# Attention visits of one unit or of two: eight heads of 256 tokens at a time from block 2 on

## The chip, the cores and the metric

The kernel runs on one core of a Trainium2 chip. Its time is the device time of one launch in microseconds (us); where several runs were timed, the median is given. A profile shows one further execution, with the start and length of each engine's instructions. The engines are TensorE (PE, with its weight loads PEld), VectorE (DVE), ScalarE (ACT), GpSimd (POOL) and SyncE (SP, which here only issues DMAs).

## What is computed

Four sequences of 768 tokens go through a retention layer of 8 heads of 64, and its output, as 3072 rows of 512, through a two-layer net with a leaky activation whose slope is learned per column.

```python
def _attn_ref(q, k, v):
    gamma = 1.0 - 2.0 ** (-5.0 - np.arange(H))
    scale = 1.0 / np.sqrt(D)
    for t in range(S):
        state = gamma[None, :, None, None] * state + np.einsum('bhd,bhe->bhde', k[:, :, t], v[:, :, t])
        y[:, :, t] = scale * np.einsum('bhd,bhde->bhe', q[:, :, t], state)

def _moe_ref(x, w_in, w_out, alpha):      # x: [3072, 512], w_in: [512, 2048], w_out: [2048, 512]
    h = x @ w_in
    g = np.maximum(h, 0.0) + alpha * np.minimum(h, 0.0)
    return g @ w_out
```

## The kernel before

**Blocks and units.** The 3072 rows are cut into 6 blocks of 512 (`n`, 0 to 5). The retention is cut into 24 *units* `w`: 256 tokens (`u = w // 2`) of four of the eight heads (`g = w % 2`: heads 0 to 3, or 4 to 7). Four units make a block. A unit has two chunks `c` of 128 tokens. `c3` is the place of the 256 tokens in their sequence (0, 1, 2).

**The dense work of a block.** `ffn1(n)` makes the first product: 16 groups of four dense products of 128x512 (L438); each group has a PSUM bank of its own, and `minus` (ScalarE, L418) and `prelu` (VectorE, L407) turn it into a 128x512 piece of `gt`. Then `ffn2(n)` makes the second: four groups of 16 products (L461), each copied out by ScalarE (`os`, L475) and written to memory by a DMA on SP's queue (L481). Both are Python generators that yield after each product, and `tick(gen, m)` emits `m` of them. The program is thus one hand-written order; the engines run their own queues in that order and wait for each other by semaphores.

**A visit.** While `ffn2(n)` runs, the retention of block n + 1 is put between its products in *visits*. `visit(w_old, w_new)` finishes one unit and begins another:

- `within(w_old)`: 16 small products (64x64 quarters of the array) of the masked scores `m2` with v into `y` (L352); then the *carried* products that add the state's share where row half and chunk are the same (L330); then a bell: a VectorE memset of one element (L365) that tells that these are through, because the other row half writes the same bank next.
- `scores(w_new)`: 16 small products of q with k into `sc` (L267); `state_sums(w_new)`: 16 (8 in the last chunk pair of a sequence) of k with v into two banks, one for each chunk (L292).
- `finish(w_old)`: the other carried products (L330), which wait for the bell; ScalarE copies y to `xT`, the next block's input (L381, 128x512).
- VectorE: `masked` multiplies the scores with the causal mask (L303, 128x1024); `state` adds the decayed state and decays again (L317, L319, 128x128 each), one pair for each chunk.

In blocks 2 to 4 there are four visits in each `ffn2`, after 16, 30, 44 and 57 of its 64 products; in block 1 there is one more, `visit(None, 8)`, after two. Block 0 has an order of its own, and block 5 has no next block.

**Preparation.** `ahead()` prepares the next unit: GpSimd scales k and q and casts v (L191, L211), SP issues the transposing DMA that gives `kq` (L204, units 8 to 23), and SP issues the loads of the unit four further on (L151). These queues keep the program's order too.

**PSUM.** Eight banks of 128x512: two "dense" banks in turn (`f`: fa, fb), two for the sums in turn (`p`: pa, pb), a pair for the scores (`s`), a pair for `y`. A unit uses half of the y pair (columns 256 to 768). `ffn1` goes round all eight in the order of a string such as "fspyfSpY"; `ffn2` uses fa and fb in turn.

Of the kernel before, what the change touches and what calls it, by code (L numbers as in the profile page):

```python
# [18 lines left out]
def kernel(  # L19
# [15 lines left out]
    nc = tc.nc  # L35
# [7 lines left out]
    WB = 4  # L43
# [96 lines left out]
    def place(w):  # L140
        u, g = divmod(w, 2)
        b, c3 = divmod(u, NUS)
        return u, g, b, c3
# [111 lines left out]
    def half(i):  # L255
        return slice(64 * i, 64 * i + 64)
# [23 lines left out]
    def chunks(w):  # L280
        return (0,) if place(w)[3] == NUS - 1 else (0, 1)
# [17 lines left out]

    def masked(w):  # L300
        kdq, kq, vx, sc = live[w]
        m2 = sbp.tile([128, 4, 2, 128], F16, tag="m2", bufs=2, name="m2")
        nc.vector.tensor_tensor(  # L303
            out=m2.rearrange("p s a i -> p s (a i)"),
            in0=sc.rearrange("p (s n) -> p s n", n=256),
            in1=mask.unsqueeze(1).to_broadcast([128, 4, 256]),
            op=MULT,
        )
        live[w][3] = m2

    def state(w, cs=None):
        u, g, b, c3 = place(w)
        decay = tab[:, 32 + 2 * g : 34 + 2 * g].unsqueeze(2).to_broadcast([128, 2, D])
        for c in cs or chunks(w):
            stv = sums.pop((w, c))[:, 0:128].rearrange("p (x e) -> p x e", e=D)
            if c3 + c > 0:
                nc.vector.tensor_tensor(out=stv, in0=tgs[2 * u + c, g], in1=stv, op=ADD)  # L317
            tg = sbp.tile([128, 4, D], F16, tag="tg", bufs=8, name="tg")[:, 0:2, :]
            nc.vector.tensor_tensor(out=tg, in0=stv, in1=decay, op=MULT)  # L319
            tgs[2 * u + c + 1, g] = tg  # L320

    def carried(w, y, started, same, after=None):
        u, g, b, c3 = place(w)
        kq = live[w][1]
        for x in range(2):
            for r in range(2):
                c = r if same else 1 - r
                if c3 + c == 0:
                    continue
                ins = nc.tensor.matmul(  # L330
                    out=y[half(x), 256 + 256 * c + 128 * r : 384 + 256 * c + 128 * r],
                    lhsT=tgs[2 * u + c, g][half(r), x, :],
                    rhs=kq[half(r), 4 + 2 * x : 6 + 2 * x, half(c)],
                    start=(c, x) not in started,
                    stop=(same == (c == r)),
                    skip_group_check=True,
                )
# [6 lines left out]
    def within(w, mid=None, teller=None, pair="y"):  # L344
        u, g, b, c3 = place(w)
        vx, m2 = live[w][2:4]
        y = ps("y", pair, 1024, FP, 1)
        started = set()
        for r in range(2):
            for a in range(2):  # L350
                for c, x in DIAG:
                    nc.tensor.matmul(  # L352
                        out=y[half(x), 256 + 256 * c + 128 * r : 384 + 256 * c + 128 * r],
                        lhsT=vx[half(c), 2 * r + x, a, :],
                        rhs=m2[half(c), 2 * r + x, a, :],
                        start=(c, x) not in started,
                        stop=(a == 1 and c3 + c == 0),
                        skip_group_check=True,
                    )
                    started.add((c, x))  # L360
        if mid:
            mid()
        last = carried(w, y, started, True)
        if teller != nc.scalar:
            done = (teller or nc.vector).memset((warm if teller is None else bell)[0:1], 0.0)  # L365
        else:
            done = teller.activation(
                out=word[0:1], in_=word[0:1], func=COPY, bias=0.0, scale=1.0
            )
        behind(done, last, "tells that the products within the chunks are through")  # L370
        live[w].append((y, started, done))

    def finish(w):
        u, g, b, c3 = place(w)
        y, started, done = live[w].pop()
        carried(w, y, started, False, done)
        live.pop(w)
        n, i = divmod(u, 2)
        if w % WB == 0:
            xT[n] = sbp.tile([128, 2, 4, 2, 128], F16, tag="xT", bufs=2, name=f"xT{n}")  # L380
        nc.scalar.activation(  # L381
            out=xT[n][:, g, 2 * i : 2 * i + 2].rearrange("p c r (i a) -> p (c r) i a", a=2),
            in_=y[:, 256:768].rearrange("p (s a i) -> p s i a", a=2, i=64),
            func=COPY,
            bias=0.0,
            scale=1.0,
        )

    def visit(w_old, w_new, cs=None, tag="p", early=False):
        if w_old is not None:  # L390
            within(w_old)
        if w_new is not None:
            scores(w_new)
            state_sums(w_new, cs, tag)
        if w_old is not None:
            finish(w_old)
        if w_new is not None and early:
            state(w_new, cs)
        if w_new is not None:
            masked(w_new)  # L400
        if w_new is not None and not early:
            state(w_new, cs)

    gts = {}

# [15 lines left out]
    def ffn1(n, order="spyfSpYf", lead=(0, 0)):  # L421


        gt = sbp.tile([128, NFT, TB], F16, tag="gt", bufs=2, name=f"gt{n}")
        gts[n] = gt
        banks = Banks(order)
        hpss = {}
        narrow, wide = lead
        steps = [(ft, hp, 0, 2) for ft in range(narrow) for hp in range(NP)]
        for hps in ((0, 1), (2, 3)):  # L430
            steps += [
                (ft, hp, 2 if ft < narrow else 0, 4) for ft in range(wide) for hp in hps
            ]
        steps += [(ft, hp, 0, 4) for ft in range(wide, NFT) for hp in range(NP)]
        for ft, hp, lo, hi in steps:
            if hp == 0 and ft not in hpss:
                hpss[ft] = banks.next("hps")
            nc.tensor.matmul(  # L438
                out=hpss[ft][:, 128 * lo : 128 * hi],
                lhsT=w_in_all[:, hp, 128 * ft : 128 * ft + 128],  # L440
                rhs=xT[n][:, hp // 2, lo:hi, hp % 2, :],
                start=(hp == 0),
                stop=(hp == NP - 1),
            )
# [41 lines left out]
    def tick(gen, m):  # L486
        for _ in range(m):
            if next(gen, 1) == 1:
                return
# [198 lines left out]
```

## Time and profile before

| | |
|---|---|
| median of three runs | 212.56 us (212.12, 212.56, 214.99) |
| the profiled execution, its own time | 211.06 us |
| its span | 209.3 us |
| instructions | 5212 |
| data moved by DMA | 38.27 MB, mean 183 GB/s |

The span is the time from the first to the last profiled instruction; a little lies around it. The profile's page gives busy times, the busy share in 40 slices, the chain of waits that ended last, and the costliest groups of instructions. The timeline lists instructions in order, those of one kind merged: start, length, engine, line, operation, names, shape and count, and in brackets the engine's idle time ahead of them and what ended it. Matmuls overlap and their ends are modelled, so distances are best taken from start to start.

### The profile page before, as it was taken

How to read it: one execution, taken by the hardware profiler on the slowest of the kernel's cores; microseconds unless marked ns; L12 is line 12 of the kernel's file. 1: busy time of each engine (PE TensorE's matmuls, PEld its weight loads, DVE VectorE, ACT ScalarE, POOL GpSimd, SP SyncE). 2: the span in 40 equal slices, each digit the busy share in tenths (PEclk: the TensorE clock that was granted, in tenths of full speed). 3: DMA queues.
4: the chain of work that ended last, by engine and by line, in shares of the span. 5: the costliest groups of instructions: out<-in, count | busy, mean ns of one | idle time of the engine just before them, and what ended most of it. 6: DMA issues, size and time to landing. Idle time of an engine off the chain costs nothing.

```text
span 209.3 us, 5212 instructions
## 1 busy us (share of the span) xinstructions
PE 202.2 (97%) x2135; PEld 101.1 (48%) x2135; DVE 126.2 (60%) x225; ACT 97.3 (47%) x166; POOL 72.9 (35%) x97
## 2 busy tenths in 40 slices
PE   7989999999999999999999999999999999999993
PEld 2655454554444555444555444555444554444452
DVE  2783986465688736688347688346788433588000
ACT  2674763274765223665223665223665223665121
POOL 0578889389945563544022454000000000000000
PEclk9999999999999999999999999999999999999999
DMA  6999999999999994991184993314500111100112
GB/s 189 336 373 359 347 397 374 369 294 312 338 280 250 229 320 114 243 318 38 53 243 114 227 285 92 99 54 107 150 0 3 50 53 50 53 0 0 50 54 96
DMA packets 64119, 38.27 MB, mean 183 GB/s; under 512 B 19152, under 2 KB 57568, under 8 KB 64096
## 3 DMA queue, kind: packets, MB, share of 16 engines
q1 hardware_dynamic: 63632, 37.69, 61.8%
q8 instruction: 16, 0.26, 0.5%
q10 hardware_dynamic: 464, 0.25, 0.5%
q14 instruction: 7, 0.06, 0.1%
HBM read 27.45 MB, written 6.29 MB: 161 GB/s over the span
## 4 chain that ended last, share of the span: by engine, by line
PE 89%; SPq 4%; DMA 3%; DVE 1%; ACT 1%; issue 1%; POOL 0%; DVEq 0%
PE hps L438 40%; PE ops L461 40%; SPq L151 4%; PE y L352 3%; DMA wi<-in_moe_w_in_dram 3%; PE sc L267 2%; PE y L330 2%; PE st L292 1%; PE trb L239 1%; DVE m L303 1%; ACT kq L245 0%; ACT os L475 0%; POOL win L181 0%; DVE tg L319 0%; DVE st L317 0%
## 5 line engine op out<-in xcount | busy, mean ns | idle before, releaser
L461 PE MATMUL ops<-wout,gt 128*128 128x512 f16 (+1 forms) x400 | 88.5, 371 | 0.3 <-ACT os L475 0.3
L438 PE MATMUL hps<-xT,win 128*128 128x512 f16 (+1 forms) x392 | 84.8, 375 | 0.3 <-POOL win L181 0.3
L407 DVE SCALAR_TENSOR_TENSOR gt<-hm,oma,hps 128x512 f16<-128x512 f32 x96 | 71.2, 747 | 21.3 <-ACT hm L418 11.6
L418 ACT ACTIVATE hm<-hps 128x512 f32<-128x512 f32 x96 | 57.0, 597 | 24.9 <-PE hps L438 24.4
L438 PEld LDWEIGHTS <-win 128*128 128x128 f16 x392 | 37.9, 98 | 45.1 <-POOL win L181 0.5
L461 PEld LDWEIGHTS <-gt 128*128 128x128 f16 x400 | 37.3, 98 | 39.8 <-issue 0.6
L191 POOL TENSOR_TENSOR kdq<-ks,tab 128x512 f16<-128x512 f32 x19 | 19.8, 1043 | 40.6 <-DMA ks<-in_k_dram 28.7
L381 ACT ACTIVATE xT<-y 128x512 f16<-128x512 f32 x24 | 14.3, 597 | 40.9 <-PE y L330 40.9
L303 DVE TENSOR_TENSOR m<-sc,mi 128x1024 f16<-128x1024 f32 x24 | 29.3, 1223 | 3.5 <-PE sc L267 1.0
L475 ACT ACTIVATE os<-ops 128x512 f32<-128x512 f32 (+2 forms) x25 | 14.2, 576 | 28.4 <-PE ops L461 28.4
L191 POOL TENSOR_TENSOR kdq<-qs,tab 128x512 f16<-128x512 f32 x22 | 23.2, 1057 | 9.1 <-DMA qs<-in_q_dram 9.1
L365 DVE MEMSET warm<- 1x1 f32 x21 | 1.2, 59 | 31.1 <-PE y L330 31.1
L245 ACT ACTIVATE kq<-trb 128x512 f16<-128x512 f16 (+1 forms) x12 | 8.6, 736 | 10.1 <-PE trb L239 10.0
L319 DVE TENSOR_TENSOR tg<-st,tab 128x128 f16<-128x128 f32 x40 | 11.6, 289 | 1.7 <-PE st L292 0.6
L330 PE MATMUL y<-kq,tg 64*64 64x128 f16 x160 | 11.4, 229 | 0.3 <-DVE warm L365 0.3
L317 DVE TENSOR_TENSOR st<-tg,st 128x128 f32<-128x128 f16 x32 | 9.3, 291 | 3.9 <-PE st L292 2.0
L352 PEld LDWEIGHTS <-vx 64*64 64x64 f16 x384 | 6.3, 106 | 9.1 <-issue 7.6
L181 POOL CAST wout<-wo 128x512 f16<-128x512 f32 x16 | 9.6, 613 | 3.0 <-DMA wo<-in_moe_w_out_dram 2.8
L211 POOL CAST vx<-vs 128x512 f16<-128x512 f32 x16 | 9.8, 610 | 2.3 <-DMA vs<-in_v_dram 2.3
L267 PE MATMUL sc<-kq 64*64 64x128 f16 x384 | 10.0, 217 | 0.5 <-ACT kq L245 0.4
L181 POOL CAST win<-wi 128x512 f16<-128x512 f32 x16 | 9.8, 613 | 1.6 <-DMA wi<-in_moe_w_in_dram 1.2
L352 PE MATMUL y<-m,vx 64*64 64x128 f16 x384 | 10.0, 221 | 0.2 <-DVE m L303 0.2
(27 smaller groups left out, 60.4 us busy)
## 6 DMA issues: line engine op xcount, KB each, us to landing
ks<-in_k_dram SPq DMA_DIRECT2D x24, 256.0 KB, 4.7
qs<-in_q_dram SPq DMA_DIRECT2D x24, 256.0 KB, 4.8
vs<-in_v_dram SPq DMA_DIRECT2D x24, 256.0 KB, 4.8
out_dram<-os SPq DMA_DIRECT2D x23, 256.0 KB, 2.9
wi<-in_moe_w_in_dram SPq DMA_DIRECT2D x16, 256.0 KB, 5.4
wo<-in_moe_w_out_dram SPq DMA_DIRECT2D x16, 256.0 KB, 5.2
kq<-kdq SPq DMA_TRANSPOSE x16, 4.3
mi<-mi_const ACTq DMA_DIRECT2D x1, 128.0 KB, 3.0
```

The source lines that it names most:

```text
L181: nc.gpsimd.tensor_copy(out=dst, in_=t)
L191: eng.tensor_tensor(out=kdq[:, kind].rearrange("p z r d -> p r z d"), in0=src.rearrange("p (r x) (a d) -> p r (x a) d", a=2, x=2), in1=tab ...
L267: nc.tensor.matmul(out=sc[half(c), at : at + 128], lhsT=kq[half(r), 2 * x + a, half(c)], rhs=kq[half(r), 4 + 2 * x : 6 + 2 * x, half(c)], ...
L303: nc.vector.tensor_tensor(out=m2.rearrange("p s a i -> p s (a i)"), in0=sc.rearrange("p (s n) -> p s n", n=256), in1=mask.unsqueeze(1).to_ ...
L330: ins = nc.tensor.matmul(out=y[half(x), 256 + 256 * c + 128 * r : 384 + 256 * c + 128 * r], lhsT=tgs[2 * u + c, g][half(r), x, :], rhs=kq[ ...
L352: nc.tensor.matmul(out=y[half(x), 256 + 256 * c + 128 * r : 384 + 256 * c + 128 * r], lhsT=vx[half(c), 2 * r + x, a, :], rhs=m2[half(c), 2 ...
L381: nc.scalar.activation(out=xT[n][:, g, 2 * i : 2 * i + 2].rearrange("p c r (i a) -> p (c r) i a", a=2), in_=y[:, 256:768].rearrange("p (s ...
L407: nc.vector.scalar_tensor_tensor(out=gt[:, ft, lo:hi], in0=hm, scalar=oma_sb[:, ft : ft + 1], in1=hps, op0=MULT, op1=ADD,)
L418: nc.scalar.activation(out=hm, in_=hps, func=RELU, bias=0.0, scale=-1.0)
L438: nc.tensor.matmul(out=hpss[ft][:, 128 * lo : 128 * hi], lhsT=w_in_all[:, hp, 128 * ft : 128 * ft + 128], rhs=xT[n][:, hp // 2, lo:hi, hp ...
L461: nc.tensor.matmul(out=opss[tq], lhsT=gt[:, ft, 128 * tq : 128 * tq + 128], rhs=w_out_all[:, ft, at], start=(ft == 0), stop=(ft == NFT - 1),)
L475: nc.scalar.activation(out=os_sb, in_=opss[tq][:, cut], func=COPY, bias=0.0, scale=1.0)
```

## The change

From block 2's retention on (units 8 to 23, placed in blocks 1 to 4), a visit holds both units of 256 tokens. `both(u_old, u_new)` takes the place of `visit`:

```diff
+    def single(g, c, r):
+        return slice(256 + 256 * c + 128 * r, 384 + 256 * c + 128 * r)
+
+    def double(g, c, r):
+        return slice(512 * c + 256 * g + 128 * r, 512 * c + 256 * g + 128 * r + 128)
...
+    def both(u_old, u_new):
+        old = [] if u_old is None else [2 * u_old, 2 * u_old + 1]
+        new = [] if u_new is None else [2 * u_new, 2 * u_new + 1]
...
+        if new:
+            u, _, b, c3 = place(new[0])
+            cs = chunks(new[0])
+            low = ps("low", "fb" if flip["f"] else "fa")
+            sums = [ps(f"sums{c}", "pa" if c == 0 else "pb") for c in range(2)]
+            beside = [t[:, 256:512] for t in sums]
+            there = through(score(new[1], ((low[:, 0:256], low[:, 256:512]), beside)))
+            m2 = [sbp.tile([128, 4, 2, 128], F16, tag="m2", bufs=4, name="m2") for _ in new]
+            masks(m2[1][:, 0:2], low)
+        if old:
+            y = ps("y", "y")
+            started = set()
+            for w in old:
+                inner(w, y, started, double)
+            for w in old:
+                last = carried(w, y, started, True, None, double)
+            done = through(last, nc.scalar)
+        if new:
+            sc = ps("sc", "s")
+            score(new[0], [[sc[:, 512 * r + 256 * x :][:, 0:256] for x in range(2)] for r in range(2)])
+            for w in new:
...
+                                ins = nc.tensor.matmul(
+                                    out=sums[c][half(r), at : at + 64],
...
+                                if there is not None:
+                                    behind(ins, there, "the other row half wrote this bank")
+                                    there = None
+        if old:
+            for w in old:
+                carried(w, y, started, False, done if w == old[0] else None, double)
+                live.pop(w)
...
+            nc.scalar.activation(
+                out=xT[n][:, 4 * i : 4 * i + 4].rearrange("p c r (i a) -> p (c r) i a", a=2),
+                in_=y.rearrange("p (s a i) -> p s i a", a=2, i=64),
...
+        if new:
+            for c in range(2):
+                masks(m2[1][:, 2 + c : 3 + c], beside[c])
+            for c in cs:
+                stv = sums[c][:, 0:256].rearrange("p (z e) -> p z e", e=D)
+                if c3 + c > 0:
+                    nc.vector.tensor_tensor(out=stv, in0=tgs[2 * u + c], in1=stv, op=ADD)
+                tgs[2 * u + c + 1] = new_state()
+                nc.vector.tensor_tensor(
+                    out=tgs[2 * u + c + 1],
+                    in0=stv,
...
+            masks(m2[0], sc)
```

The scores of heads 4 to 7 (`new[1]`) come first in the visit: one row half's go to `low`, the dense bank that `ffn2` isn't filling at that time, the other's to the free halves of the two banks of the sums (`beside`). Two row halves write these banks one after the other, and a second bell (`there`, VectorE) stands between them. The y pair now holds both units. `through` is the bell, cut out of `within`; the one behind the first carried products is ScalarE's (`word`, a copy of one element). `carried` and `inner` (the 16 products of `within`) place their output by `at`. The masks are four instructions (128x512, twice 128x256, 128x1024), the state's steps are 128x256, and y's copy is 128x1024.

The state `tg` of both units stands in one tile, in block 0 and 1 too; `m2` has four buffers instead of two. `xT` is a tile [128, 8, 2, 128]; from block 2 on it has the 128 tokens ahead of the heads' half:

```diff
-            xT[n] = sbp.tile([128, 2, 4, 2, 128], F16, tag="xT", bufs=2, name=f"xT{n}")
+            xT[n] = new_x(n)
...
-                rhs=xT[n][:, hp // 2, lo:hi, hp % 2, :],
+                rhs=xT[n].rearrange(
+                    "p (g t) r i -> p g t r i" if n < 2 else "p (t g) r i -> p g t r i", g=2
+                )[:, hp // 2, lo:hi, hp % 2, :],
```

The order in blocks 1 to 4:

```diff
-        gen = ffn1(n, "fspyfSpY" if n > 1 else "spyfSpYf")
+        gen = ffn1(n, "fyfpsYpS" if n > 1 else "spyfSpYf")
...
-        w0 = WB * (n + 1)
-        if n == 1:
-            tick(gen, 2)
-            visit(None, w0)
+        u0 = 2 * (n + 1)
         if n + 1 < NBLK:
-            for i in range(1, WB):
-                tick(gen, 10 if n > 1 and i == 1 else 8)
-                if i == 2:
-                    ahead()
-                tick(gen, 6)
-                visit(w0 + i - 1, w0 + i)
-            tick(gen, 6)
+            tick(gen, 8)
+            if n == 1:
+                both(None, u0)
             ahead()
-            tick(gen, 7)
-            visit(w0 + WB - 1, w0 + WB if w0 + WB < NW else None)
+            ahead()
+            tick(gen, 28 if n == 1 else 12)
+            both(u0, u0 + 1)
+            tick(gen, 21 if n == 1 else 33)
+            both(u0 + 1, u0 + 2 if 2 * u0 + 4 < NW else None)
```

In block 1 the visits stand after 8, 36 and 57 of the 64 products of `ffn2`, in blocks 2 to 4 after 20 and 53. TensorE has the same products before and after, 4271 instructions in all; VectorE has 16 fewer.

More of the change, by code (lines that the diff above doesn't have):

```diff
@@ L301, in masked @@
         kdq, kq, vx, sc = live[w]
-        m2 = sbp.tile([128, 4, 2, 128], F16, tag="m2", bufs=2, name="m2")
+        m2 = sbp.tile([128, 4, 2, 128], F16, tag="m2", bufs=4, name="m2")
         nc.vector.tensor_tensor(
@@ L309, in masked, with new_state @@
         live[w][3] = m2
+    def new_state():
+        return sbp.tile([128, 4, D], F16, tag="tg", bufs=8, name="tg")
     def state(w, cs=None):
@@ L315, in state, with carried @@
             stv = sums.pop((w, c))[:, 0:128].rearrange("p (x e) -> p x e", e=D)
+            gs = slice(2 * g, 2 * g + 2)
             if c3 + c > 0:
[L317 to L322, printed above, removed]
+                nc.vector.tensor_tensor(out=stv, in0=tgs[2 * u + c][:, gs], in1=stv, op=ADD)
+            if 2 * u + c + 1 not in tgs:
+                tgs[2 * u + c + 1] = new_state()
+            nc.vector.tensor_tensor(out=tgs[2 * u + c + 1][:, gs], in0=stv, in1=decay, op=MULT)
+    def single(g, c, r):
+        return slice(256 + 256 * c + 128 * r, 384 + 256 * c + 128 * r)
+    def double(g, c, r):
+        return slice(512 * c + 256 * g + 128 * r, 512 * c + 256 * g + 128 * r + 128)
+    def carried(w, y, started, same, after=None, at=single):
         u, g, b, c3 = place(w)
@@ L330, in carried @@
                 ins = nc.tensor.matmul(
-                    out=y[half(x), 256 + 256 * c + 128 * r : 384 + 256 * c + 128 * r],
-                    lhsT=tgs[2 * u + c, g][half(r), x, :],
+                    out=y[half(x), at(g, c, r)],
+                    lhsT=tgs[2 * u + c][half(r), 2 * g + x, :],
                     rhs=kq[half(r), 4 + 2 * x : 6 + 2 * x, half(c)],
@@ L342, in carried, with inner @@
         return ins
-    def within(w, mid=None, teller=None, pair="y"):
+    def inner(w, y, started, at=single):
         u, g, b, c3 = place(w)
         vx, m2 = live[w][2:4]
-        y = ps("y", pair, 1024, FP, 1)
-        started = set()
         for r in range(2):
@@ L352, in within @@
                     nc.tensor.matmul(
-                        out=y[half(x), 256 + 256 * c + 128 * r : 384 + 256 * c + 128 * r],
+                        out=y[half(x), at(g, c, r)],
                         lhsT=vx[half(c), 2 * r + x, a, :],
@@ L360, in within, with through @@
                     started.add((c, x))
-        if mid:
-            mid()
-        last = carried(w, y, started, True)
+    def through(last, teller=None):
         if teller != nc.scalar:
@@ L370, in within, with new_x @@
         behind(done, last, "tells that the products within the chunks are through")
-        live[w].append((y, started, done))
+        return done
+    def within(w, mid=None, teller=None, pair="y"):
+        y = ps("y", pair, 1024, FP, 1)
+        started = set()
+        inner(w, y, started)
+        if mid:
+            mid()
+        last = carried(w, y, started, True)
+        live[w].append((y, started, through(last, teller)))
+    def new_x(n):
+        return sbp.tile([128, 8, 2, 128], F16, tag="xT", bufs=2, name=f"xT{n}")
     def finish(w):
@@ L379, in finish @@
         if w % WB == 0:
-            xT[n] = sbp.tile([128, 2, 4, 2, 128], F16, tag="xT", bufs=2, name=f"xT{n}")
+            xT[n] = new_x(n)
         nc.scalar.activation(
-            out=xT[n][:, g, 2 * i : 2 * i + 2].rearrange("p c r (i a) -> p (c r) i a", a=2),
+            out=xT[n].rearrange("p (g t) r i -> p g t r i", g=2)[:, g, 2 * i : 2 * i + 2].rearrange("p c r (i a) -> p (c r) i a", a=2),
             in_=y[:, 256:768].rearrange("p (s a i) -> p s i a", a=2, i=64),
```

45 lines of the change are left out of this document (added).

## The prediction

> **What bounds the kernel now.** I read the page first (busy times, slices, chain of waits), then the timeline of TensorE, because the chain lies on it.
>
> ```profile
> PE 202.2 (97%) x2135; PEld 101.1 (48%) x2135; DVE 126.2 (60%) x225; ACT 97.3 (47%) x166; POOL 72.9 (35%) x97
> PE   7989999999999999999999999999999999999993
> PEclk9999999999999999999999999999999999999999
> PE 89%; SPq 4%; DMA 3%; DVE 1%; ACT 1%; issue 1%; POOL 0%; DVEq 0%
> PE hps L438 40%; PE ops L461 40%; SPq L151 4%; PE y L352 3%; DMA wi<-in_moe_w_in_dram 3%; PE sc L267 2%; PE y L330 2%; PE st L292 1%; PE trb L239 1%; DVE m L303 1%; ACT kq L245 0%; ACT os L475 0%; POOL win L181 0%; DVE tg L319 0%; DVE st L317 0%
> ```
>
> TensorE is busy in every slice at the full granted clock; the chain is 89% TensorE, 80% of it dense products (L438, L461). So the end moves by whatever TensorE's stream gains or loses. The change keeps every dense product and every small one; it only moves the small ones together. What a visit costs *beyond its products* is thus the question, and the timeline answers it. Here are a visit that only takes scores and sums (block 1), a full visit (block 3) and the last one (block 4), with the dense runs around them.
>
> ```profile
> 65.74 0.59 PE L461 MATMUL ops<-wout,gt 128*128 128x512 f16 x2
> 66.26 0.42 PE L267 MATMUL sc<-kq 64*64 64x128 f16 x16
> 66.51 0.29 PE L292 MATMUL st<-vx,kdq 64*64 64x64 f16 x16
> 66.74 3.19 PE L461 MATMUL ops<-wout,gt 128*128 128x512 f16 x14
> ...
> 133.53 3.20 PE L461 MATMUL ops<-wout,gt 128*128 128x512 f16 x14
> 136.65 0.42 PE L352 MATMUL y<-m,vx 64*64 64x128 f16 x16
> 136.90 0.23 PE L330 MATMUL y<-kq,tg 64*64 64x128 f16 x4
> 136.96 0.39 PE L267 MATMUL sc<-kq 64*64 64x128 f16 x16
> 137.18 0.29 PE L292 MATMUL st<-vx,kdq 64*64 64x64 f16 x16
> 137.31 0.25 PE L330 MATMUL y<-kq,tg 64*64 64x128 f16 x4
> 137.50 3.20 PE L461 MATMUL ops<-wout,gt 128*128 128x512 f16 x14
> ...
> 145.19 1.68 PE L461 MATMUL ops<-wout,gt 128*128 128x512 f16 x7
> 146.72 13.98 PE L438 MATMUL hps<-xT,win 128*128 128x512 f16 x64
> ...
> 173.73 2.10 PE L461 MATMUL ops<-wout,gt 128*128 128x512 f16 x9
> 175.77 0.42 PE L352 MATMUL y<-m,vx 64*64 64x128 f16 x16
> 176.02 0.23 PE L330 MATMUL y<-kq,tg 64*64 64x128 f16 x4
> 176.43 0.25 PE L330 MATMUL y<-kq,tg 64*64 64x128 f16 x4 [0.19 <-DVE warm L365]
> 176.61 1.68 PE L461 MATMUL ops<-wout,gt 128*128 128x512 f16 x7
> ```
>
> The pitch of dense products is (13.98 − 3.20) / (64 − 14) = 0.2156 us, in both dense stages. A visit costs the distance of two dense runs less the dense products between them: 137.50 − 133.53 − 14 × 0.2156 = 0.95 us for a full one; 66.74 − 65.74 − 2 × 0.2156 = 0.57 for the first, which has no old unit; 176.61 − 173.73 − 9 × 0.2156 = 0.94 for the last, which has no new one. From block 1 on there are 17: one, fifteen and one, 0.57 + 15 × 0.95 + 0.94 = 15.76 us. That is the whole sum on which the change can work.
>
> **What a visit holds.** By starts: the next dense product would have begun at 133.53 + 14 × 0.2156 = 136.55, the first y begins at 136.65: 0.10 to get in. Then y 0.25, carried 0.06, scores 0.22, sums 0.13, and 0.19 from the second carried group to the next dense product. Sixteen products of 128 columns cost 0.22 where nothing switches (scores), so four cost 0.055; y's first group has 0.03 too much, and getting out costs 0.19 − 0.055 = 0.135. So 0.265 us of a visit is a price of going there and back, and 0.685 is its products.
>
> The Trainium skill (TensorEngine Tiling (Array Packing), Key Properties) says that changing the tiling mode drains TensorE. Taken strictly, the first y would begin at 136.73, where the dense run ends, and the dense run after it at 137.56; the trace has 136.65 and 137.50, so by these modelled ends the drain is not a whole one. By the rule the price would be 0.14 more, 0.405.
>
> **The change, part by part.** After it there are nine visits in place of 17: one with new units only, seven full, one with old units only. All the products stay, so eight times 0.265 = 2.12 us go. Against that stand waits within the visit, which I price from these rows:
>
> ```profile
> 14.88 0.25 PE L330 MATMUL y<-kq,tg 64*64 64x128 f16 x4
> 15.25 0.20 ACT L367 ACTIVATE word<-word 1x1 f32<-1x1 f32 x1 [0.64 <-PE y L330]
> ...
> 137.20 0.06 DVE L365 MEMSET warm<- 1x1 f32 x1 [2.02 <-PE y L330]
> 146.92 0.60 ACT L475 ACTIVATE os<-ops 128x512 f32<-128x512 f32 x1 [0.98 <-PE ops L461]
> ...
> 31.59 1.02 ACT L245 ACTIVATE kq<-trb 128x1024 f16<-128x1024 f16 x1
> 63.98 3.34 DVE L407 SCALAR_TENSOR_TENSOR gt<-hm,oma,hps 128x512 f16<-128x512 f32 x4
> L303 DVE TENSOR_TENSOR m<-sc,mi 128x1024 f16<-128x1024 f32 x24 | 29.3, 1223 | 3.5 <-PE sc L267 1.0
> L319 DVE TENSOR_TENSOR tg<-st,tab 128x128 f16<-128x128 f32 x40 | 11.6, 289 | 1.7 <-PE st L292 0.6
> ```
>
> *The bell before the second carried products.* It was a VectorE memset: carried at 136.90, memset at 137.20, second carried group at 137.31, 0.41 from product to release; scores and sums (0.055 + 0.22 + 0.13) just cover it. Now ScalarE rings: 0.30 to 0.37 to its start (137.20 − 136.90; 15.25 − 14.88), 0.20 long, and 0.05 to the release (0.41 − 0.30 − 0.06): 0.55 to 0.62. The cover grows too, to 0.055 + 0.22 + 2 × 0.13 = 0.535. I take 0.07 of waiting in each of the seven full visits, 0.49; the ends are 0.02 and 0.15, the latter were the sums to hide nothing more. On TensorE the second carried group and all dense products stand behind it, which is why it counts in full; ScalarE has only the copy of y behind it, which needs those products anyway.
>
> *The new bell ("there") before the sums.* In the seven full visits y and carried (0.55) lie between it and the sums: nothing. In the first visit only one unit's scores do: 0.41 − 0.055 − 0.22 = 0.135. On VectorE the masks stand behind it, and they need the same scores.
>
> *The last visit* has nothing between its bell and the second carried group: 0.94, plus one more y and two more carried groups (0.33), plus the slower bell (0.14 to 0.21, I take 0.18) = 1.45.
>
> *The first visit*: 0.57 + another unit's scores and sums (0.35) + 0.135 = 1.06.
>
> *The sum*: a full visit 2 × 0.685 + 0.265 + 0.07 = 1.705. 1.06 + 7 × 1.705 + 1.45 = 14.45 us against 15.76: 1.31 us gained.
>
> *Scores in the free dense bank.* They wait for the copy that empties it. The last product of the run at 145.19 starts at 146.48; its copy runs from 146.92 to 147.52, 1.04 later. Where a visit stands four products into the next group (blocks 1 to 4, once each), the scores would start 5 × 0.2156 + 0.10 = 1.18 after that product: 0.14 of room less 0.05 for the release, so nothing; its end is 0.1 each. Elsewhere five or more have gone by. In block 1's first visit the bank is that of the last prelu, whose four end at 67.32; the scores come at 65.74 + 8 × 0.2156 + 0.10 = 67.56.
>
> *VectorE.* From 128 to 1024 columns its products with the mask or decay grow by (1.223 − 0.289) / 896, so 0.42 for 256 columns. After the sums, two masks, four state steps and the mask of 1024 are 6 × 0.42 + 1.22 = 3.74, ending some 5.4 us after the visit's start (1.35 for scores to sums, 0.3 to start). The nearest next visit is 1.705 + 21 × 0.2156 = 6.2 later, and its y 0.35 after that: 1.1 us of room. The first prelu after a visit is due 1.705 + 7 × 0.2156 + 4 × 0.2156 + 1.04 = 5.1 in: 0.3 late at worst, and eight dense banks in turn hide it, as prelus take 3.34 / 4 = 0.835 where the products bring one each 0.862. Fewer, wider state steps cost VectorE less in all.
>
> *ScalarE's copy of y* takes 1.02 for 1024 columns in place of two of 0.60 (512 columns at 146.92); the next dense stage needs it 1.5 us after the visit in the nearest case (7 × 0.2156): 0.3 of room.
>
> *xT's new order* has the moving operand in four pieces of 128 as before, only twice as far apart: nothing (a rival below).
>
> *The queues.* Two units must now be prepared ahead of a visit, so SP's transposes of two units with six loads pass ahead of the writes of the first groups. GpSimd's order is the same. Output writes come later, six buffers cover a block's four. The transposes:
>
> ```profile
> 66.38 1.69 SPq L204 DMA_TRANSPOSE kq<-kdq  x1
> ...
> 71.55 1.40 SPq L204 DMA_TRANSPOSE kq<-kdq  x1
> ...
> 74.25 0.50 SPq L151 DMA_DIRECT2D vs<-in_v_dram  x1
> ...
> 80.81 1.31 SPq L204 DMA_TRANSPOSE kq<-kdq  x1
> ...
> DMA to landing us min/median/max: 2.7/4.3/5.6
> ...
> 51.80:83.90 32.10, 32.10 (x369) 15.64 (x368) 21.64 (x39) 14.66 (x25) 18.23 (x21) 1.00 1.01 254
> ```
>
> These three are units 11, 12 and 13 of the sixteen transposed so. Unit 13's was issued at 80.81, behind two writes; block 1's third visit now needs it at 65.74 + 57 × 0.2156 + 1.06 + 1.705 = 80.8. In the new order it follows the loads after unit 12's, the last of them issued by 74.25 + 0.50: it starts at 74.8, or sooner, as a write that stood before them comes later, and lands at 79.1 by the median, 80.4 by the longest. Unit 11 lands by 72.0 and is needed at 74.6. Later blocks have more room. So nothing, but the DMA engines are full in that block (1.01).
>
> **The number.** 211.06 (the profiled execution) − 1.31 = 209.75. The median of the three runs is 212.56, 1.0071 of it: 211.2. With no new wait the gain is 2.1 (210.4), with the upper ends (7 × 0.15, 4 × 0.1) 0.35 (212.2): this case's own range. About 2% (4.25 us) is what a measurement of this kernel can tell from no change, and the forecast is well inside.
>
> **Rivals.**
>
> *Whole drains.* Visits cost what the strict rule says, 0.14 more each: eight removed give 1.1 more, 210.1. For it: every end of a product is modelled. Against: 0.95 was measured from starts, and no room for 0.14 is in it. 4%.
>
> *Unit 13 comes late.* For: full DMA engines, room of 0.4 to 1.7 us. Each microsecond past 80.8 costs one, once; from 82.1 on the gain is gone. 211.4 to 213. 13%.
>
> *VectorE's chain becomes the bound* in a visit, y waiting for the 1024 mask placed last. 1.1 us of room speaks against; it would cost up to 0.5 in each of seven visits: 211.5 to 214.7. 6%.
>
> *Slower: the moving operand.* If pieces 1 KB apart read slower than 512 B apart, all 256 dense products of the first stage in blocks 2 to 5 pay. 5 ns each undo the gain, 22 ns (a tenth of the pitch) make 5.6 − 1.3 = 4.3 more: 216.9. Against: today's four pieces have the same pitch as the whole rows of the second stage. 7%.
>
> The forecast has 70%. Faster than 208.3 no case gives (all of 8 × 0.265 is 1%); 3% for what I can't see. Slower than 216.8: the moving operand and a rest, 8%. Within: 89%. The range takes in the late transposes and the whole drains: 209.8 to 213.2.
>
> **What would show it.** Nine visits; full ones of about 1.7 us, dense pitch unchanged at 0.2156; idle before the second carried group under 0.1, in the last visit about 0.5; the first visit's sums waiting 0.13; blocks 2 and 3 shorter by about 0.4 each. Wrong if L557's pitch differs from L582's, if y or the first scores of a visit show waits for VectorE, ScalarE or a DMA, or if full visits cost 1.9, the price of two.

## The result, and the profile after

The changed kernel takes 210.86 us in the median of 20 runs, the kernel before 211.87 in 20 runs beside it: a ratio of 0.9926 with a 95% interval of 0.9903 to 0.995, 0.7% or 1.6 us faster. The ratio leaves out runs more than 1.5% above the fastest of their kernel (two of the changed kernel, one of the other); the quotient of the two medians over all runs is 0.9952, 1.0 us. The prediction was 211.2.

The page of the changed kernel, its span, busy times and chain of waits:

```profile
span 209.1 us, 5197 instructions
PE 201.5 (96%) x2135; PEld 101.5 (49%) x2135; DVE 123.2 (59%) x209; ACT 97.9 (47%) x166; POOL 72.8 (35%) x97
PE 88%; SPq 4%; DMA 3%; DVE 1%; ACT 1%; issue 1%; POOL 0%; DVEq 0%; ACTq 0%
```

The profiled execution took 211.09 us, no less than the 211.06 of the one before. That is no contradiction, and it must be seen before anything is compared: block 1 begins at different times. The timeline of TensorE, first before, then after:

```profile
51.83 14.07 PE L438 MATMUL hps<-xT,win 128*128 128x512 f16 x64
```

```profile
53.21 14.07 PE L557 MATMUL hps<-xT,win 128*128 128x512 f16 x64
67.12 1.89 PE L582 MATMUL ops<-wout,gt 128*128 128x512 f16 x8
...
69.18 0.39 PE L437 MATMUL sc<-kq 64*64 64x128 f16 x16
69.66 0.44 PE L481 MATMUL sums<-vx,kdq 64*64 64x64 f16 x32
70.03 6.22 PE L582 MATMUL ops<-wout,gt 128*128 128x512 f16 x28
...
83.37 0.42 PE L481 MATMUL sums<-vx,kdq 64*64 64x64 f16 x32
83.69 0.31 PE L340 MATMUL y<-kq,tg 64*64 64x128 f16 x8
83.92 1.69 PE L582 MATMUL ops<-wout,gt 128*128 128x512 f16 x7
...
130.18 4.48 PE L582 MATMUL ops<-wout,gt 128*128 128x512 f16 x20
...
134.84 0.62 PE L360 MATMUL y<-m,vx 64*64 64x128 f16 x32
135.29 0.28 PE L340 MATMUL y<-kq,tg 64*64 64x128 f16 x8
135.40 0.39 PE L437 MATMUL sc<-kq 64*64 64x128 f16 x16
135.62 0.42 PE L481 MATMUL sums<-vx,kdq 64*64 64x64 f16 x32
135.88 0.31 PE L340 MATMUL y<-kq,tg 64*64 64x128 f16 x8
136.12 7.30 PE L582 MATMUL ops<-wout,gt 128*128 128x512 f16 x33
...
147.29 13.98 PE L557 MATMUL hps<-xT,win 128*128 128x512 f16 x64
...
174.26 0.64 PE L360 MATMUL y<-m,vx 64*64 64x128 f16 x32
174.74 0.28 PE L340 MATMUL y<-kq,tg 64*64 64x128 f16 x8
175.38 0.31 PE L340 MATMUL y<-kq,tg 64*64 64x128 f16 x8 [0.37 <-ACT word L374]
175.62 2.55 PE L582 MATMUL ops<-wout,gt 128*128 128x512 f16 x11
```

The opening, which the change hardly touches, was 1.4 us longer here; from block 1's first product to the last product of all, TensorE took 153.86 us before and 152.36 after, 1.50 less. In nine of the ten profiles of this study block 1 began between 51.7 and 53.6 us, whatever the kernel, a spread larger than the gain. (In the tenth, that of the round trip by itself, it began at 56.5: the granted clock was 0.51 from 17.2 to 24.1 us there.) So the visits themselves are compared. The full one above costs 136.12 − 130.18 − 20 × 0.2156 = 1.63 by its rows. The table takes the unrounded starts, from the last dense product ahead of a visit to the first behind it, less one pitch: 1.615 for this one.

| kernel | first visit | full visits | last visit | all, us |
|---|---|---|---|---|
| before | 0.57 | 15 of 0.92 to 0.94 | 0.94 | 15.52 |
| after | 1.19 | 7 of 1.60 to 1.68 | 1.45 | 14.11 |

The visits became 1.42 us cheaper, and 1.42 / 211.87 is 0.67% of the 0.74% measured. The rest of the 1.50 lies just behind the visits: the first pitch of the dense run there is 0.226 us in place of 0.216, in both kernels, and eight of these 0.01 went too. Otherwise the dense pitch is what it was: 64 products in 13.98 us in either kernel.

### The profile page after: what moved, and what is told of

Read it like the earlier page. It is cut to its first block, busy times and chain, and to the rows that moved or that the text cites. A ratio compares the mean times of both kernels' runs of the same rounds, so it can differ in the third digit from the quotient of the medians.

```text
span 209.1 us, 5197 instructions
## 1 busy us (share of the span) xinstructions
PE 201.5 (96%) x2135; PEld 101.5 (49%) x2135; DVE 123.2 (59%) x209; ACT 97.9 (47%) x166; POOL 72.8 (35%) x97
## 4 chain that ended last, share of the span: by engine, by line
PE 88%; SPq 4%; DMA 3%; DVE 1%; ACT 1%; issue 1%; POOL 0%; DVEq 0%; ACTq 0%
PE hps L557 40%; PE ops L582 39%; SPq L151 4%; DMA wi<-in_moe_w_in_dram 3%; PE y L360 2%; PE y L340 2%; PE low L437 1%; PE sums L481 1%; PE sc L437 1%; PE trb L239 1%; DVE m L303 1%; ACT kq L245 0%; PE sc L267 0%; ACT os L596 0%; PE st L292 0%
## 5 line engine op out<-in xcount | busy, mean ns | idle before, releaser
L582 PE MATMUL ops<-wout,gt 128*128 128x512 f16 (+1 forms) x400 | 87.2, 371 | 0.3 <-ACT os L596 0.3
L582 PEld LDWEIGHTS <-gt 128*128 128x128 f16 x400 | 37.9, 98 | 41.4 <-issue 0.6
L447 DVE TENSOR_TENSOR m<-low,mi 128x512 f16<-128x512 f32 x8 | 5.5, 686 | 24.8 <-issue 24.0
L303 DVE TENSOR_TENSOR m<-sc,mi 128x1024 f16<-128x1024 f32 x8 | 9.8, 1222 | 0.8 <-PE sc L267 0.4
L498 ACT ACTIVATE xT<-y 128x1024 f16<-128x1024 f32 x8 | 8.2, 1023 | 3.3 <-PE y L340 3.3
L447 DVE TENSOR_TENSOR m<-sc,mi 128x1024 f16<-128x1024 f32 x8 | 9.7, 1214 | 0.0
L340 PE MATMUL y<-kq,tg 64*64 64x128 f16 x160 | 8.5, 224 | 0.5 <-ACT word L374 0.4
L360 PE MATMUL y<-m,vx 64*64 64x128 f16 x384 | 8.3, 218 | 0.2 <-DVE m L303 0.2
L219 PE MATMUL trb<-ones 128*128 128x512 f16 (+1 forms) x21 | 6.5, 434 | 1.5 <-DVE word L624 1.4
L374 ACT ACTIVATE word<-word 1x1 f32<-1x1 f32 x11 | 2.2, 201 | 12.1 <-PE y L340 12.1
```

The lines of the kernel that those rows point to most:

```text
L303: nc.vector.tensor_tensor(out=m2.rearrange("p s a i -> p s (a i)"), in0=sc.rearrange("p (s n) -> p s n", n=256), in1=mask.unsqueeze(1).to_ ...
L340: ins = nc.tensor.matmul(out=y[half(x), at(g, c, r)], lhsT=tgs[2 * u + c][half(r), 2 * g + x, :], rhs=kq[half(r), 4 + 2 * x : 6 + 2 * x, h ...
L360: nc.tensor.matmul(out=y[half(x), at(g, c, r)], lhsT=vx[half(c), 2 * r + x, a, :], rhs=m2[half(c), 2 * r + x, a, :], start=(c, x) not in s ...
L447: nc.vector.tensor_tensor(out=dst.rearrange("p s a i -> p s (a i)"), in0=src.rearrange("p (s n) -> p s n", n=256), in1=mask.unsqueeze(1).t ...
L582: nc.tensor.matmul(out=opss[tq], lhsT=gt[:, ft, 128 * tq : 128 * tq + 128], rhs=w_out_all[:, ft, at], start=(ft == 0), stop=(ft == NFT - 1),)
```

## The experiments

### One dense product put into the middle of a visit

```diff
             done = through(last, nc.scalar)
+        if mid:
+            mid()
         if new:
...
-            both(u0, u0 + 1)
-            tick(gen, 21 if n == 1 else 33)
+            one = lambda: tick(gen, 1)
+            both(u0, u0 + 1, one)
+            tick(gen, 20 if n == 1 else 32)
```

> In each of the seven full visits one dense product is moved from behind the visit to its middle, between the bell behind the first carried products and the second scores. Nothing else changes: same products, same banks, same positions of the visits, same order on the other engines. Theory (a visit costs its products and a price for going there and back): the extra round trip adds its 0.25 to 0.27 us to each full visit, less the wait for ScalarE's bell that the inserted product covers (about 0.06 in three of the seven), so full visits go from 1.60 to 1.68 us up to about 1.87, and the time rises by some 1.7 us: ratio to the kernel before about 1.000 (0.997 to 1.003), the gain is gone. Rival (the gain comes from fewer or wider instructions on VectorE and ScalarE, or from the earlier preparation): they are all as in the changed kernel, so full visits stay below 1.72 and the ratio stays at about 0.993.

The ratio was 0.9993 (0.9954 to 1.0031): the gain is gone. From block 1's first product to the last, TensorE took 153.63 us. One such visit in the timeline:

```profile
130.31 3.83 PE L584 MATMUL ops<-wout,gt 128*128 128x512 f16 x17
...
134.32 0.62 PE L360 MATMUL y<-m,vx 64*64 64x128 f16 x32
134.76 0.28 PE L340 MATMUL y<-kq,tg 64*64 64x128 f16 x8
134.98 0.39 PE L584 MATMUL ops<-wout,gt 128*128 128x512 f16 x1
135.30 0.42 PE L437 MATMUL sc<-kq 64*64 64x128 f16 x16
```

The single dense product starts 0.22 after the carried products, and the scores start 0.32 after it, 0.10 more than a pitch. The two parts of the full visits cost 1.00 and 0.82, together 1.82 against 1.60 to 1.68; all visits 15.38. VectorE and ScalarE had the same instructions as in the changed kernel, so fewer or wider instructions there don't give the gain.

### The round trip by itself

Products that nobody waits for, in the last block, where there are no visits (the kernel then computes them besides its own work):

```diff
+            def quarter(m):
+                for i in range(m):
+                    r, c = DIAG[i % 4]
+                    nc.tensor.matmul(
+                        out=banks[r][half(c), 0:128], lhsT=ones[half(r), 0:64],
+                        rhs=ones[half(r), 0:128], start=True, stop=True,
+                    )
...
+            for put, m in ((quarter, 4), (quarter, 16), (quarter, 32), (whole, 4), (whole, 16), (quarter, 4), (quarter, 16)):
+                tick(gen, 7)
+                put(m)
```

> The price of a round trip by itself. The changed kernel, with groups of products that nobody reads put into the last block's second dense stage, where no visits are: after each 7 dense products, in this order, 4, 16 and 32 products of 64x64 quarters with 128 columns, then 4 and 16 of the whole 128x128 array with 128 columns, then 4 and 16 quarters once more. No engine waits for them and they wait for nothing. Theory (the price belongs to the change between whole array and quarters): quarters cost 0.014 us each and 0.255 on top whatever their number: 0.31, 0.48 and 0.70 us, and again 0.31 and 0.48; whole ones cost 0.056 each and nothing on top: 0.22 and 0.89. Rival (any interruption of the dense stream by short products costs it): the whole ones have about 0.25 on top too, 0.47 and 1.15. Second rival (the price in a visit comes from waits on other engines and banks): quarters have next to nothing on top, 0.06, 0.22 and 0.45.

By unrounded starts, taken as in the table, 4, 16 and 32 quarters cost 0.275, 0.443 and 0.667, and the second 4 cost 0.276. That is 0.056 for each four, and 0.22 on top whatever their number. (The last 16 stand beside a dense product of 256 columns, and cost 0.445 with its shorter pitch.) The price expected was 0.255. The whole-array products cost 0.223 and 0.893, nothing on top. The rows around the groups of 4, 16 and 32 quarters, of which only the first product is shown, and of 4 whole products:

```profile
195.10 1.67 PE L582 MATMUL ops<-wout,gt 128*128 128x512 f16 x7
196.71 0.24 PE L779 MATMUL ra<-ones 64*64 64x128 f16 x1
...
196.89 1.69 PE L582 MATMUL ops<-wout,gt 128*128 128x512 f16 x7
...
198.85 1.68 PE L582 MATMUL ops<-wout,gt 128*128 128x512 f16 x7
...
201.04 1.68 PE L582 MATMUL ops<-wout,gt 128*128 128x512 f16 x7
202.56 0.39 PE L786 MATMUL ra<-ones 128*128 128x128 f16 x4
202.78 1.67 PE L582 MATMUL ops<-wout,gt 128*128 128x512 f16 x7
```

The longer first pitch shows here as well: seven dense products take 1.68 to 1.69 behind quarters and 1.67 behind whole products; by unrounded starts the first pitch is 0.226 to 0.227 against 0.216. Counted in, a round trip costs 0.23.

So the price is that of going from the whole array to quarters and back, and no other engine is needed for it. The rule on changing the tiling mode that the prediction quoted from the Trainium skill (TensorEngine Tiling (Array Packing), Key Properties) agrees in kind: a change of the mode costs, a shorter product doesn't. Its size is 0.22, not the 0.405 that the prediction worked out for whole drains.

### Everything but the merging

```diff
-        m2 = sbp.tile([128, 4, 2, 128], F16, tag="m2", bufs=2, name="m2")
+        m2 = sbp.tile([128, 4, 2, 128], F16, tag="m2", bufs=4, name="m2")
...
-        gen = ffn1(n, "fspyfSpY" if n > 1 else "spyfSpYf")
+        gen = ffn1(n, "fyfpsYpS" if n > 1 else "spyfSpYf")
...
-                if i == 2:
+                if i == 1:
                     ahead()
+                    ahead()
                 tick(gen, 6)
                 visit(w0 + i - 1, w0 + i)
-            tick(gen, 6)
-            ahead()
-            tick(gen, 7)
+            tick(gen, 13)
```

> The kernel before with everything that the change does around the visits and without their merging: four buffers for the masked scores, the changed kernel's order of the banks in the first dense stage, and both preparations of a block's second stage issued early, one behind the other, so that transposes and loads pass ahead of the writes. Visits, their number (17) and their instructions are those of before. Theory: none of this lies on TensorE's path, so full visits stay at 0.92 to 0.94 us and the ratio is 1.000 (0.997 to 1.003). Rival (earlier preparation or looser buffers give the gain): the ratio is about 0.993, or at least clearly below 1.

The ratio was 1.0002 (0.9973 to 1.0031), full visits 0.92 to 0.94, all 15.50. Looser buffers, the other order of the banks and the early preparation give nothing by themselves. (xT's order, the common state tile and ScalarE's bell were not in this run.)

### VectorE's bell, and the mask behind it

```diff
             there = through(score(new[1], ((low[:, 0:256], low[:, 256:512]), beside)))
...
-            masks(m2[1][:, 0:2], low)
         if old:
...
-            done = through(last, nc.scalar)
+            done = through(last)
         if new:
+            masks(m2[1][:, 0:2], low)
```

> The changed kernel with the bell before the second carried products rung by VectorE, as before the change, in place of ScalarE, and the mask of the free dense bank moved behind that bell on VectorE. Theory (what is left in a visit besides products and round trip is ScalarE's slower bell): release 0.41 us after the last of the first carried products' group in place of 0.53 to 0.59: full visits all at 1.60 to 1.62, those of 1.66 to 1.68 included, and the last visit 1.25 in place of 1.45; the first stays at 1.19. In all 0.4 us less in the visits, too little for the time of one run to show. Rival (the second visits of the blocks are longer for another reason, such as more columns or a bank that isn't free): they stay at 1.66 to 1.68 though the bell is earlier.

Full visits took 1.578 to 1.593, all seven, a little less than expected, the last 1.27 and the first 1.19; all 13.56. The longer second visits of the blocks were the bell, then. In the changed kernel's trace, ScalarE's timeline, the two sorts differ before the bell is rung: in block 1 TensorE's last carried group starts at 76.93 and 83.09, and ScalarE's bell 0.28 and 0.34 later.

```profile
77.21 0.20 ACT L374 ACTIVATE word<-word 1x1 f32<-1x1 f32 x1 [1.19 <-PE y L340]
...
83.43 0.20 ACT L374 ACTIVATE word<-word 1x1 f32<-1x1 f32 x1 [2.33 <-PE y L340]
```

The later sort waits for two engines (TensorE, and ScalarE's own earlier write), and ScalarE runs a separate semaphore instruction of 0.017 us ahead of it; the first sort waits for TensorE alone and has none. So it is in all eight of these bells: four start 0.26 to 0.27 after the last carried product, and the four with the semaphore instruction 0.32 to 0.33.

### A version without the waits

Besides VectorE's bell and the mask behind it, the first visit puts the scores of heads 4 to 7 into the y pair, which no old unit needs there, and the last visit has one dense product before its second carried group.

```diff
+            if old:
+                low = ps("low", "fb" if flip["f"] else "fa")
+                beside = [t[:, 256:512] for t in sums]
+                there = through(score(new[1], ((low[:, 0:256], low[:, 256:512]), beside)))
+            else:
+                pair, there = ps("y", "y"), None
+                score(new[1], [[pair[:, 512 * r + 256 * x :][:, 0:256] for x in range(2)] for r in range(2)])
...
-            done = through(last, nc.scalar)
+            done = through(last)
+        if mid:
+            mid()
...
+            both(u0 + 1, None if last else u0 + 2, (lambda: tick(gen, 1)) if last else None)
```

> The changed kernel less the waits that its trace still shows in the visits. VectorE rings the bell before the second carried products, the mask of the free dense bank behind it (as in the run with that bell alone, where full visits took 1.578 to 1.593 us); the first visit puts the scores of heads 4 to 7 into the y pair, which is free there, so it needs no bell before its sums; one dense product stands before the second carried products in the last visit, which costs a round trip of 0.22 and covers the 0.38 of waiting that VectorE's bell left there. Theory (a visit costs its products, 0.22 for each round trip, and what its bells don't hide): first visit 0.70 + 0.22 = 0.92 (was 1.19), full ones 1.58 to 1.59 (were 1.60 to 1.68), the last 0.67 + 0.44 = 1.11 (was 1.45); all visits together 13.1 us against 14.1 in the changed kernel and 15.5 in the kernel before; ratio to the kernel before 0.9886 (0.985 to 0.992). Rival (the waits move elsewhere, since VectorE takes up its masks later): the visits shrink but dense products behind them wait for VectorE, and the ratio stays at 0.993.

The ratio was 0.99 (0.9865 to 0.9934). The visits came out as expected: first 0.92, full 1.58 to 1.59, last 0.78 + 0.34 = 1.12, all 13.14. The last visit:

```profile
174.03 0.64 PE L360 MATMUL y<-m,vx 64*64 64x128 f16 x32
174.50 0.28 PE L340 MATMUL y<-kq,tg 64*64 64x128 f16 x8
174.72 0.39 PE L591 MATMUL ops<-wout,gt 128*128 128x512 f16 x1
175.03 0.31 PE L340 MATMUL y<-kq,tg 64*64 64x128 f16 x8
```

A round trip more is worth it here, since it stands in place of a longer wait: the idle time of 0.37 before the second carried group is gone.

### A transposed tile that comes late

```diff
             ahead()
-            ahead()
+            if n > 1:
+                ahead()
...
-            tick(gen, 21 if n == 1 else 33)
+            tick(gen, 13 if n == 1 else 33)
+            if n == 1:
+                ahead()
+                tick(gen, 8)
```

> The changed kernel with one preparation of block 1 put later: that of unit 13 comes after the third output group of the block, so SP issues its transposes only behind the write of that group, some 0.7 us before block 1's third visit in place of 6 us before it. Theory (the transposes' landing is the nearest other bound, and each microsecond past the visit's start costs one): issue about 81.3 in the changed kernel's time scale, landing 4.3 to 6.1 us later as its transposes took there, visit due at 82.3: TensorE waits 3.3 to 5.1 us for the transposed tile ahead of that visit, once, and the end comes as much later: some 214 to 216 us. Rival (a late tile is taken up by the room behind, as the dense stages can go on): TensorE's order is fixed and has nothing to put in, so no; if it did, the time would stay at 211.

One run took 213.67 us, a little below the 214 to 216 expected. SP issued unit 13's transposes at 80.41, and they landed 3.38 later, quicker than expected; the DMA share meanwhile was 0.88, against 1.18 between issue and landing in the changed kernel, which is a likely reason but not a tested one. The timeline of TensorE, and its granted clock (PEclk) in three stretches:

```profile
83.84 0.31 PE L437 MATMUL low<-kq 64*64 64x128 f16 x1 [2.58 <-DMA kq<-kdq]
...
84.26 1.07 PE L360 MATMUL y<-m,vx 64*64 64x128 f16 x32
85.11 0.43 PE L340 MATMUL y<-kq,tg 64*64 64x128 f16 x8
```

```profile
core 0: us, PE busy (x) PEld busy (x) DVE busy (x) ACT busy (x) POOL busy (x), PEclk, DMA share, GB/s
78.00:81.00 3.00, 3.00 (x16) 1.26 (x13) 1.20 (x2) 0.60 (x1) 1.54 (x2) 1.00 0.72 251
81.00:83.80 2.80, 0.26 (x2) 0.00 (x0) 0.00 (x0) 0.00 (x0) 0.61 (x1) 0.94 0.99 196
83.80:86.50 2.70, 2.66 (x112) 2.54 (x112) 0.74 (x3) 0.20 (x1) 1.07 (x2) 0.50 0.91 269
```

TensorE waited 2.65 us, less than the 3.3 to 5.1 expected, and the visit cost 5.45 in place of 1.68, 3.77 more. The missing 1.1 is the visit itself: its 32 y products take 0.85 to the next group's start where 0.45 is usual, since the clock granted after the wait was half. The first pitch behind the visit was 0.37 in place of 0.23 as well, so from block 1's first product to the last one TensorE took 156.27 us, 3.9 more than in the changed kernel. So the theory's direction held and its price was wrong: this wait cost more than itself.

### The changed kernel and the version without the waits, once more

No new edit: both ran on one chip, beside the same runs of the kernel before.

> The changed kernel itself once more, on the same chip and beside the same runs as the version without the waits, since their intervals against the kernel before overlap. Its visits took 14.11 us in the first profile, 1.42 less than in the kernel before; ratio 0.9933 by that alone. Theory (the opening up to block 1 varies by more than a microsecond from run to run and has nothing to do with the change): the visits take 14.1 us again, wherever block 1 begins.

> The version without the waits once more, beside the changed kernel on the same chip. Theory: visits 13.14 us as before, 0.97 less than the changed kernel's, so its ratio to the kernel before is 0.9886 and lies 0.004 to 0.005 below the changed kernel's of this call; the intervals of this call may still overlap, as each is about 0.004 wide to either side. Rival (the earlier bell and later masks cost something that the visits do not show): both ratios are the same.

The ratios were 0.9933 (0.9898 to 0.9967) and 0.9883 (0.984 to 0.9926). The version without the waits had visits of 13.14 again. It is 0.0050 below the changed kernel here; its first ratio, 0.99, was 0.0026 below the changed kernel's first; the intervals overlap, so the times alone don't part the two, the visits in the traces do.

In one visit of the changed kernel the expectation failed. Block 1 began at 51.70 here, 1.5 us earlier than in the first profile, and its third visit took 1.98, all visits 14.41:

```profile
81.14 0.24 PE L437 MATMUL low<-kq 64*64 64x128 f16 x1 [0.24 <-DMA kq<-kdq]
```

TensorE waits for unit 13's transposed tile; the scores begin 0.31 later than usual. The answer for the transposes in this run and in the first profile of the changed kernel:

```profile
L204 SPq DMA_TRANSPOSE kq<-kdq x2: 1359/2014/2670, 72.1 to 75.4; - x2
DMA to landing us min/median/max: 3.9/4.8/5.7
```

```profile
L204 SPq DMA_TRANSPOSE kq<-kdq x1: 1786/1786/1786, 75.8 to 75.8; - x1
DMA to landing us min/median/max: 6.1/6.1/6.1
```

It was issued at 75.4 and landed at 81.1; in the first profile it was issued at 75.8, landed at 81.9 and was wanted at 82.3. The early opening brought the visit forward by more than the transposes, so the wait showed. A quick opening alone doesn't bring it: with one dense product in the middle of the visits block 1 began at 51.98, and the transposes, issued at 73.9, were in time. None of the other five profiles with this order of the queue has the wait; the one with the round trip by itself runs the changed kernel's visits, and they took 14.11.

## Why the prediction was right

**The bound.** TensorE's stream set the end before and after, and the visits' 1.42 us are nearly all of the gain. Right, and shown from both sides: one dense product in the middle of the merged visits takes the gain away, and buffers, order of banks and early preparation without the merging give none.

**Eight round trips.** Predicted 8 × 0.265 = 2.12. A round trip measured by itself costs 0.22, and 0.23 with the longer pitch behind it, so 1.84. The term was too large by a wait that it held. The prediction had scores and sums just cover VectorE's bell in a single visit, but in all sixteen visits with an old unit the second carried group's first weights start 0.11 after the memset, so the bell set their time there. A single visit has products for 0.685 and a trip for 0.22, 0.905 in all, and took 0.92 to 0.94: by difference the bell cost some 0.03. That wait went with the single visits; the merged ones have waits of their own, in the next terms. The 15.76 of the 17 visits against the table's 15.52 is mostly the longer first pitch, which the prediction's rows hold and the table leaves out.

**ScalarE's bell.** Predicted 0.07 in each full visit, 0.49. Without waits a full visit is 2 × 0.685 + 0.22 = 1.59. It took 1.60 to 1.62 in the blocks' earlier visits and 1.66 to 1.68 in the later ones, 0.33 over in all, a third less than predicted; that there are two sorts was not seen.

**The bell before the first visit's sums.** Predicted 0.135, measured 1.19 − 0.70 − 0.22 = 0.27. The sums' first weight load waits for two engines, VectorE and GpSimd, and TensorE runs a semaphore instruction of 0.051 us ahead of it: the release came 0.18 after the memset's start in place of 0.11. The memset came 0.02 later than in the rows of before, and the first sum 0.03 after its weights, where a carried product follows at once.

**The last visit.** Predicted 1.45, measured 1.45. The idle time before its second carried group was 0.37: the 0.19 of before and the 0.18 of the sum, not the "about 0.5" named as a sign.

**The sum.** 1.31 predicted, 1.50 measured: the trips were 0.28 less than their term, and the waits, net of those that went, 0.34 in place of 0.81. Both sizes were too large, one for the gain and one against it, and they partly cancel. That 211.2 comes so near the measured 210.86 is partly luck: it was reckoned from a median of 212.56 over three runs, where 20 gave 211.87.

**VectorE and ScalarE.** From block 1 on no product waited for the masks or the copy of y. In block 1 the second visit's mask of 1024 columns begins at 79.14 and takes 1.21, and the third visit's y begins at 82.59: 2.2 us of room there.

```profile
79.14 1.21 DVE L447 TENSOR_TENSOR m<-sc,mi 128x1024 f16<-128x1024 f32 x1
82.59 0.62 PE L360 MATMUL y<-m,vx 64*64 64x128 f16 x32
```

The first prelu after that visit starts 0.03 after its ScalarE half (87.14 against 86.51 + 0.60), so it wasn't late at all.

**xT's order.** Dense products of the first stage have the same pitch before and after, 0.2158 by unrounded starts. That rival is out.

**Unit 13.** The step that failed is its landing, predicted at 79.1 to 80.4: with the DMA engines full it was issued at 75.4 to 75.8, not 74.8, and took 5.7 to 6.1, at and beyond the longest seen before. The rival's mechanism is real: the first scores of a visit waiting for a DMA was one of the prediction's own signs of being wrong. Its price was 0.31 us in one of three profiles of these visits, far from undoing the gain.

**Whole drains.** Out: 0.22, or 0.23 with the longer pitch, was measured alone, and visits without waits are 1.58 to 1.59.

## What to carry to other kernels

Where small products stand between dense ones on a full TensorE, price the visit in three parts: its products, a fixed price for going to the other tiling and back, and the waits that its own small products don't cover; fewer, larger visits save only the second, and may give it back in the third. A dense product in the middle of a visit is worth its round trip only where a longer wait stands there. Compare such kernels by that part of the trace, as an opening that varies by more than the gain hides it in the total.

## What the runs showed of the hardware that was not expected

A wait on two engines cost more than a wait on one. Behind a bell of the same 0.059 us, a weight load with one wait started 0.11 us after the memset's start, one with two waits 0.18 after it, with a semaphore instruction of 0.051 in between. ScalarE's bells show it too: 0.32 to 0.33 against 0.26 to 0.27.

The first pitch of a dense run behind quarters is 0.226 us in place of 0.216, behind every visit at the full clock and in the round trip by itself; behind whole-array products of 128 columns it is 0.216. Why is not shown.

TensorE's clock halved after a short idle time. The Trainium skill (TensorE: Matmul & The Clock Gate, Part 1) has it fall to half after an idle window of about 3.4 us. Here 2.58 us of idle were enough: the granted clock was 0.94 in the stretch with the wait and 0.50 in the 2.7 us behind it, so a wait of 2.65 us cost 3.9. The length of the gap alone doesn't decide it. In the profile of the round trip by itself the clock was 0.51 from 17.2 to 24.1 us, though from 8 us on no gap ahead of that had been longer than 0.74. In the first profile of the version without the waits a gap of 1.27 that ended at 17.2 us left it at 1.00. What decides it stays open here.
